# Linear attention and two MLPs on one core: the first attention's steps in one written order, the exponential table fetched at the start

## The chip, the cores and the metric

The kernel runs as one program on one core of a Trainium2 chip. The metric is the device time of one execution in microseconds. Three executions of the kernel before took 1090.41, 1093.3 and 1094.17 us; the median, 1093.3 us, is the time that the change is compared with.

## What is computed

Four batches, 8 heads, 576 positions, head dimension 64, 128 features. Cut to what matters:

```
def phi(x):
    proj = einsum('bhsd,df->bhsf', x, w_phi)
    proj = proj - max(abs(proj), axis=-1, keepdims=True)
    return concatenate([exp(proj), exp(-proj)], axis=-1)
q_p, k_p = phi(q), phi(k)
kv  = einsum('bhsf,bhsd->bhfd', k_p, v)
z   = sum(k_p, axis=2)
num = einsum('bhsf,bhfd->bhsd', q_p, kv)
den = einsum('bhsf,bhf->bhs', q_p, z)[..., None] + 1e-6
x   = (num / den) as (2304, 512)
h   = x @ w_in                      # 512 -> 2048
x   = maximum(0.01 * h, h) @ w_out  # 2048 -> 512
g   = x @ w_gate                    # 512 -> 1536
out = (g * sigmoid(g) * (x @ w_val)) @ w_out2
```

## The kernel before

The work goes batch by batch (b = 0 to 3). A batch's attention gives `x` of 512 rows and 576 columns, held as a rounded part `xh` and a rest `xl`; both MLPs then run on these columns as a list of units, each a group of matmuls for one block of 128 features. The attention of batch b+1 is spread between the units of batch b. Only the attention of batch 0 has nothing beside it but the first conversions of weights: it is the opening, and the change is about it alone.

A head pair j (four of them) is two heads side by side. In the opening the keys of a pair are handled as three groups of key tiles (two, two and one tile of 128 positions), twelve groups p = 0 to 11 in all. For each, TensorE projects the keys (`first_k`, L431), VectorE takes the largest absolute value (L441) and subtracts it (L442, recorded at the helper `sub`, L60), ScalarE makes both exponentials (L446, L447), and TensorE multiplies them with the values and ones (`k_back`, L225) into one bank that sums a pair. ScalarE copies that bank out (`k_z`, `kvh`).

The queries of a pair are handled in two halves t of 288 columns, eight groups g = 2j + t. For each, TensorE projects both heads (`q_p`, L339) and VectorE takes the largest absolute value within blocks, transposed (L344). Then the maximum is turned by TensorE (`q_m_t`, L356), reduced, split in two parts and spread over the rows by VectorE (L361 to L369), subtracted by a matmul into the projection's bank (`q_exp`, L379), and ScalarE makes both exponentials (L381, L382). `q_num` multiplies with `kvh` on TensorE (L399) and copies the denominators on ScalarE (L402). `q_fin` transposes them, takes the reciprocal, transposes back, multiplies (VectorE, L407 to L417), casts to `xh` on ScalarE (L69) and subtracts for `xl` on VectorE (L60).

The order of these steps is made in two stages. `first_steps` gives each piece a time on a scale of its own and emits the pieces in that order; then the scheduler, which works with estimated times, orders the instructions of each engine once more. Only those that carry the token "opening" keep the order in which they were emitted: the exponentials, the copies and casts by `cp`, the denominators, and one step of each weight's conversion (L570), all on ScalarE. TensorE and VectorE follow the scheduler.

A weight arrives as 64-bit numbers and is converted by two steps on ScalarE and three on VectorE (three and two for the second MLP): an absolute value with a scale (L570), a conversion of the low half (L572), shift, merge and add on VectorE (L580, L581, L586), then a rounded part by ScalarE (L596) and the rest by VectorE (L60). Raw weights and the first MLP's converted weights share five buffers named `wi`. Four weights, those of the first four units, are converted in the opening (`split_first`). After it `split_next` converts about two a unit.

The loads of keys, queries and constants go through SP's queue, w_phi and the values of the first two head pairs through ScalarE's. Each loading engine issues in order. Names in the views: `raw` and `pk` are keys and queries, `xh` and `xl` at first also values, `wo` the key features, `mk` their maxima, `pm` and `pa` banks of PSUM, `acc` the maxima spread over rows, `dn` the denominators, `es` a tile for constants and later for results of units. The matmuls of units have line 660.

Of the kernel before, what the change touches and what calls it, by code (L numbers as in the profile page):

```python
# [17 lines left out]
P = 128  # L18
# [21 lines left out]


@with_exitstack
def linear_attention_two_mlps(ctx: ExitStack, tc, qT, kT, vt, w_phi, w1, w2, wg, wv, w3, cst, out):
# [15 lines left out]
    def sub(o, a, b):  # L59
        dve.tensor_tensor(out=o, in0=a, in1=b, op=ALU.subtract)  # L60
# [3 lines left out]
    def in_opening(i):  # L64
        if opening[0]:
            tc.stamp_issue_order_token(i.ins, "opening")

    def cp(o, a):
        in_opening(act.activation(o, a, AF.Copy))  # L69
# [22 lines left out]
    def query_constants():  # L92
        s = signs.pop()
        for t in mm:
            dve.tensor_scalar(out=t, in0=s[:, 0, 0:32], scalar1=0.0, scalar2=None, op0=ALU.mult)
        dve.tensor_scalar(out=ones, in0=s[:, 0], scalar1=0.0, scalar2=1.0, op0=ALU.mult, op1=ALU.add)
        dve.tensor_copy(sel, s)
# [11 lines left out]
    def warm_up():  # L109
        zero = T([P, 2 * F], F32, "es", 5)  # L110
        pool.memset(zero, 0.0)
        ps = bk(0)
        for i in range(5):
            pe.matmul(ps[:, 0 : 2 * F], zero[:, 0:F], zero, start=True, stop=True)
# [15 lines left out]
    def load_k(b, j):  # L130
        raw["k", b, j] = t = T([P, S], F32, *(("pk", 5) if b == 0 and j > 1 else ("raw", 2)))
        if b or j:
            nc.sync.dma_start(out=t, in_=kT[b, j])
        else:
            nc.scalar.dma_start(out=wbd.rearrange("p h f -> p (h f)"), in_=w_phi)
            for c in (slice(0, 256), slice(256, S)):
                nc.sync.dma_start(out=t[:, c], in_=kT[b, j][:, c])
        if whole(b):
            for s in range(0, NST, 2):
# [4 lines left out]
                q = nc.scalar if b == 0 and j < 2 else nc.sync  # L144
                q.dma_start(out=t[:, :, :, 0, :], in_=vt[b, j, :, s : s + n])
# [19 lines left out]
    def v_split(b, j):  # L165
# [4 lines left out]
        for st in (slice(0, 2), slice(2, NST)):  # L170
            i = act.activation(t[:, st, :, 0, :], v[:, st], AF.Copy)
            tc.stamp_issue_order_token(i.ins, "opening")
            sub(t[:, st, :, 1, :], v[:, st], t[:, st, :, 0, :].bitcast(F32))

    def k_front(b, j, s):
# [12 lines left out]
        mk = T([P, 2], F32, "mk", 2)  # L188
# [27 lines left out]
    def k_back(b, j, s):  # L216
# [4 lines left out]
        if whole(b):  # L221
            v = vaug.pop((b, j, s))
            for h in range(2):
                for a in range(2):
                    pe.matmul(  # L225
# [6 lines left out]
                    )  # L232
            return
        v = vhl[b, j][:, s]
        for h in range(2):
            for i, part in enumerate((fh, fl)):
                pe.matmul(  # L237
# [6 lines left out]
                )  # L244
# [85 lines left out]

    def q_p(b, j, t):

        c = slice(HT * t, HT * t + HT)
        m = tops[t][:, 0 : 2 * NB].rearrange("p (h k) -> p h k", h=2)
        for h in range(2):
            bank = pt[b, j, h, t] = bk(b)
            ps = bank[:, 0:HT]
            if b == 0:
                pe.matmul(ps, wbd[:, h], raw["q", b, j][:, c], start=True, stop=True)  # L339
            else:  # L340
                a = qs[b, j][h][:, c]
                pe.matmul(ps, wst_h, a, start=True, stop=False)
                pe.matmul(ps, wst_l, a, start=False, stop=True)
            dve.tensor_reduce(  # L344
                out=m[:, h],
                in_=ps.rearrange("p (k i) -> p k i", i=32),
                axis=AX.X,
                op=ALU.max,
                apply_absolute_value=True,
                apply_transpose=True,  # L350
            )

    def q_m_t(b, j, t):

        turned = pt[b, j, 1, t][:, HT : HT + P]
        pe.matmul(  # L356
            turned, tops[t], ident, is_transpose=True, start=False, stop=True, skip_group_check=True
        )
        turned = turned[0 : 2 * NB]
        top = T([2 * NB, 32], F32, "top", 2)  # L360
        dve.tensor_reduce(out=top, in_=turned.rearrange("r (g i) -> r i g", g=4), axis=AX.X, op=ALU.max)  # L361
        x = mm[t]
        hi = x[0 : 2 * NB]
        dve.tensor_copy(hi, top)
        sub(x[32 : 32 + 2 * NB], top, hi.bitcast(F32))
        if t == 0:
            mrow[b, j] = T([P, 2 * NB, 32], F32R, *(("mrow", 1) if b else ("acc", 4)))
        r = mrow[b, j][:, NB * t : NB * t + NB]
        dve.tensor_tensor(  # L369
            out=r,  # L370
            in0=x.bitcast(F32).rearrange("p (o i) -> p o i", o=1).to_broadcast([P, NB, 32]),
            in1=mask.rearrange("p (k o) -> p k o", o=1).to_broadcast([P, NB, 32]),
            op=ALU.mult,
        )

    def q_exp(b, j, h, t):
        ps = pt.pop((b, j, h, t))[:, 0:HT]
        r = mrow[b, j][:, NB * t : NB * t + NB].rearrange("p k i -> p (k i)")
        pe.matmul(ps, sel[:, h], r, start=False, stop=True, skip_group_check=True)  # L379
        f = T([P, 2, HT], F32, "ff" if b else ("ff", "fh", "fl")[(2 * t + h + j) % 3], 3)  # L380
        in_opening(act.activation(f[:, 0], ps, AF.Exp))  # L381
        in_opening(act.activation(f[:, 1], ps, AF.Exp, scale=-1.0))  # L382
# [8 lines left out]
    def q_num(b, j, h, t):  # L391
# [6 lines left out]
        for i, (w, x) in enumerate(ops):  # L398
            pe.matmul(ps, w, x, start=(i == 0), stop=(i == len(ops) - 1))  # L399
        if h == 0:  # L400
            dn[b, j, t] = T([P, HT], F32, "dn", 2)
        in_opening(act.activation(dn[b, j, t][D * h : D * h + D], ps[D:P], AF.Copy, bias=1e-6))  # L402

    def q_fin(b, j, t):
        d = dn.pop((b, j, t))
        t1 = T([P, HT // 32, 32], F32, "t1", 1)
        dve.transpose(out=t1.rearrange("p a b -> p (a b)"), in_=d)  # L407
        rc = T([P, HT // 32, 1], F32, "rc", 1)
        dve.reciprocal(out=rc, in_=t1[:, :, 0:1])
        rb = T([P, HT // 32, 32], F32, "rb", 1)  # L410
        dve.transpose(out=rb, in_=rc.to_broadcast([P, HT // 32, 32]))
        rb = rb.rearrange("p a b -> p (a b)")
        x = T([P, HT], F32, "xf", 1)
        for h in range(2):
            o = slice(D * h, D * h + D)
            ps = qn.pop((b, j, h, t))
            dve.tensor_tensor(out=x[o], in0=ps[0:D, 0:HT], in1=rb[o], op=ALU.mult)  # L417
# [4 lines left out]
        cp(xh[b, j][:, c], x)  # L422
        sub(xl[b, j][:, c], x, xh[b, j][:, c].bitcast(F32))
# [3 lines left out]
    def first_k(j, s, n):  # L427
        ps = bk(0)
        for i in range(n):
            o = slice(OFF[s + i], OFF[s + i] + P)  # L430
            pe.matmul(  # L431
                ps[:, 2 * F * i : 2 * F * i + 2 * F],
                raw["k", 0, j][:, o],
                wbd.rearrange("p h f -> p (h f)"),
                start=(i == 0),
                stop=(i == n - 1),
                skip_group_check=True,
            )
        pv = ps[:, 0 : 2 * F * n].rearrange("p (r f) -> p r f", f=F)
        mk = T([P, 2 * n], F32, "mk", 2)  # L440
        dve.tensor_reduce(out=mk, in_=pv, axis=AX.X, op=ALU.max, apply_absolute_value=True)  # L441
        f = T([P, n, 2, 2, F], F32, "wo", 5)  # L442
        d = f.rearrange("p n h a f -> p (n h) a f")
        m = mk.rearrange("p (r o) -> p r o", o=1).to_broadcast([P, 2 * n, F])
        sub(d[:, :, 1], pv, m)
        in_opening(act.activation(d[:, :, 0], d[:, :, 1], AF.Exp))  # L446
        in_opening(act.activation(d[:, :, 1], d[:, :, 1], AF.Exp, scale=-1.0))  # L447
        for i in range(n):
            ff[0, j, s + i] = f[:, i]

    def first_back(j, s, n):
        for i in range(n):
            k_back(0, j, s + i)
        if s + n == NST:
            k_z(0, j)

    def first_steps():

        events = []

        def at(time, fn, *args):
            events.append((time, len(events), lambda: fn(*args)))

        for i, (j, s, n) in enumerate(pairs):
            at(i, first_k, j, s, n)
            at(i + 1.4, first_back, j, s, n)
        for g in range(2 * NP):
            j, t = divmod(g, 2)
            base = 2 + 1.3 * g
            last = max(base + 2.05, 3 * j + 3.5 + 0.4 * t)  # L470
            at(base + 0.1, q_p, 0, j, t)
            at(base + 0.7, q_m_t, 0, j, t)
            for h in range(2):
                at(base + 1.25 + 0.1 * h, q_exp, 0, j, h, t)
                at(last + 0.2 * h, q_num, 0, j, h, t)
            at(last + 0.25, q_fin, 0, j, t)
        steps = [[] for _ in range(int(max(e[0] for e in events)) + 1)]
        for time, _, fn in sorted(events, key=lambda e: e[:2]):
            steps[int(time)].append(fn)
        return steps  # L480
# [80 lines left out]
    def w_to_f32(key):  # L561


# [6 lines left out]
        i = act.activation(t, high.bitcast(F32), AF.Abs, scale=REBIAS)  # L570
        tc.stamp_issue_order_token(i.ins, "opening")
        act.activation(low, low.bitcast(U32), AF.Copy, scale=2.0**-29)  # L572
        if key[0] in "gv3":

            act.activation(high, high.bitcast(F32), AF.Prelu, scale=2.0**-20, alpha=2.0**100)
            dve.scalar_tensor_tensor(
                out=ti, in0=ti, scalar=3, in1=high, op0=ALU.logical_shift_left, op1=ALU.bitwise_or
            )
# [626 lines left out]
```

## Time and profile before

| what | value |
|---|---|
| median of three executions | 1093.3 us |
| the profiled execution | 1097.21 us |
| its span, first to last instruction | 1095.3 us |
| mean granted TensorE clock (1.00 is full) | 0.983 |
| TensorE busy | 1059.4 us, 97% |
| VectorE busy | 798.1 us, 73% |
| ScalarE busy | 650.7 us, 59% |

The views are these. The page gives busy time by engine and by group of instructions. The windows give each engine's busy time in a stretch, with the number of instructions (x), and the granted clock. The waits say who stood idle for whom: total, number of times, longest. The timeline lists instructions by start and duration; a bracket gives the idle time before one and what ended it. PE is TensorE, DVE VectorE, ACT ScalarE, POOL GpSimd; ACTq and SPq are the queues that issue transfers. A matmul leaves two records in most of these views, so a count of records is twice a count of matmuls where the operands are of full fp32.

### The profile page before, as it was taken

The numbers are of one execution on the slowest core, as the hardware profiler recorded it, in microseconds if no ns is written. First come the engines' busy times: TensorE is split into PE (matmuls) and PEld (weight loads), VectorE is DVE, ScalarE is ACT, GpSimd is POOL, SyncE is SP. The second block draws the span as 40 slices with busy tenths as digits, with TensorE's granted clock in tenths as the row PEclk, the third lists the DMA queues.
The fourth block names the chain that finished last, engine by engine and source line by source line (L and its number), as shares of the span: only waits on it lengthen the run. The fifth ranks groups of instructions, "written<-read, shape, count | busy, mean of one in ns | idle before, by whom it ended". The sixth has DMA issues, their size and how long they took to land.

```text
span 1095.3 us, 20408 instructions
## 1 busy us (share of the span) xinstructions
PE 1059.4 (97%) x7642; PEld 1031.3 (94%) x7642; DVE 798.1 (73%) x1730; ACT 650.7 (59%) x1443; POOL 21.8 (2%) x57
## 2 busy tenths in 40 slices
PE   8779899999999999999999999999999999999998
PEld 7658899998989999999999999999999999999998
DVE  4665888999888988868776865858878742368473
ACT  4436988789896788846553366755444234336441
POOL 1000010000000000000000000000000000000000
PEclk9889899999999999999999999999999999999999
DMA  8102887656775697776463375536968757657542
GB/s 246 36 22 76 327 291 239 213 197 233 231 247 165 238 354 291 279 294 224 155 232 127 134 280 211 193 119 253 322 242 311 281 171 277 239 173 265 197 148 89
DMA packets 101492, 236.19 MB, mean 216 GB/s; under 512 B 19857, under 2 KB 35985, under 8 KB 101393
## 3 DMA queue, kind: packets, MB, share of 16 engines
q1 hardware_dynamic: 94560, 219.41, 57.4%
q0 software_dynamic: 4032, 14.68, 3.6%
q8 instruction: 61, 1.00, 0.4%
q10 hardware_dynamic: 2800, 0.79, 0.3%
q14 instruction: 39, 0.31, 0.1%
HBM read 169.30 MB, written 65.54 MB: 214 GB/s over the span
## 4 chain that ended last, share of the span: by engine, by line
PE 80%; DMA 6%; DVE 4%; ACT 2%; issue 1%; SPq 0%; DVEq 0%; ACTq 0%
PE pm L660 56%; PE pa L786 8%; PE pm L786 4%; PE pa L399 3%; PE pa L184 2%; PE pa L237 2%; PE pa L225 1%; DMA wi<-in_w_dram 1%; DMA wi<-in_wg_dram 1%; DMA wo<-parts 1%; DMA wi<-parts 1%; DMA wr<-kept 1%; DMA sums<-wr 1%; DMA vhl<-parts 1%; PE pa L379 0%
## 5 line engine op out<-in xcount | busy, mean ns | idle before, releaser
L660 PE MATMUL pm<-xh,wi 128*128 128x288 f32 x1664 | 353.7, 299 | 3.3 <-DVE wi L60 1.1
L660 PE MATMUL pm<-gp,wo 128*128 128x288 f32 x2256 | 340.5, 298 | 0.9 <-ACT gp L69 0.4
L660 PEld LDWEIGHTS pm<-gp,wo 128*128 128x128 f32 x2256 | 313.8, 189 | 3.3 <-ACT gp L69 1.4
L660 PEld LDWEIGHTS pm<-xh,wi 128*128 128x128 f32 x1664 | 273.0, 189 | 6.7 <-DVE wi L60 1.9
L660 PE MATMUL pm<-xl,wi 128*128 128x288 f32 x832 | 247.1, 298 | 0.0
L660 PEld LDWEIGHTS pm<-xl,wi 128*128 128x128 f32 x832 | 157.4, 189 | 0.4
L727 DVE TENSOR_TENSOR acc<-pm,acc 128x288 f32<-128x288 f32 x160 | 69.9, 451 | 48.0 <-PE pm L660 47.2
L60 DVE TENSOR_TENSOR gp<-es,gp 128x576 fp32r<-128x576 f32 x94 | 70.5, 750 | 25.9 <-ACT gp L69 25.2
L69 ACT ACTIVATE gp<-es 128x576 fp32r<-128x576 f32 x94 | 64.7, 690 | 28.4 <-DVE es L708 23.2
L60 DVE TENSOR_TENSOR wi<-wr,wi 128x512 fp32r<-128x512 f32 x96 | 65.1, 683 | 14.1 <-ACT wi L596 13.4
L596 ACT ACTIVATE wi<-wr 128x512 fp32r<-128x512 f32 x96 | 60.2, 638 | 21.0 <-DVE wr L60 5.3
L786 PE MATMUL pm<-xh,wi 128*128 128x288 f32 x272 | 62.6, 296 | 1.8 <-ACT xg L69 0.8
L60 DVE TENSOR_TENSOR fl<-ff,fh 128x512 fp32r<-128x512 f32 (+1 forms) x72 | 51.1, 712 | 10.2 <-ACT fh L69 9.8
L572 ACT ACTIVATE wi<-wi 128x512 int32<-128x512 uint32 x68 | 46.4, 685 | 17.7 <-DMA wi<-in_wg_dram 9.4
L570 ACT ACTIVATE wr<-wi 128x512 f32<-128x512 f32 x68 | 46.4, 683 | 15.6 <-DMA wi<-in_w_dram 5.8
L586 DVE TENSOR_TENSOR wr<-wr,wi 128x512 uint16<-128x512 uint16 x68 | 51.4, 755 | 1.2
L786 PEld LDWEIGHTS pm<-xh,wi 128*128 128x128 f32 x272 | 46.4, 188 | 2.9 <-DVE mk L189 1.1
L402 ACT ACTIVATE dn<-pa 64x288 f32<-64x288 f32 x64 | 26.0, 406 | 38.7 <-PE pa L399 37.8
L69 ACT ACTIVATE fh<-ff 128x512 fp32r<-128x512 f32 (+1 forms) x72 | 47.4, 664 | 0.9
L688 ACT ACTIVATE es<-pm 128x288 f32<-128x288 f32 x72 | 29.7, 421 | 24.4 <-PE pm L786 16.5
L69 ACT ACTIVATE acc<-pm 128x288 f32<-128x288 f32 x64 | 26.2, 417 | 26.5 <-PE pm L660 26.5
L708 DVE SCALAR_TENSOR_TENSOR es<-pm,es 128x288 f32<-128x288 f32 x72 | 31.9, 447 | 12.8 <-PE pm L660 12.3
(212 smaller groups left out, 2087.0 us busy)
## 6 DMA issues: line engine op xcount, KB each, us to landing
wo<-parts SPq DMA_DIRECT2D x77, 512.0 KB, 6.2
wi<-parts SPq DMA_DIRECT2D x68, 512.0 KB, 5.5
parts<-wi SPq DMA_DIRECT2D x56, 512.0 KB, 4.4
wi<-in_w_dram SPq DMA_DIRECT2D x44, 512.0 KB, 5.3
wr<-kept SPq DMA_DIRECT2D x64, 256.0 KB, 4.2
parts<-wo POOLq DMA_DIRECT2D x28, 512.0 KB, 5.7
kept<-wr SPq DMA_DIRECT2D x40, 256.0 KB, 4.5
wi<-in_wg_dram SPq DMA_DIRECT2D x12, 512.0 KB, 4.6
```

Source lines behind the costliest of these rows:

```text
L60: dve.tensor_tensor(out=o, in0=a, in1=b, op=ALU.subtract)
L69: in_opening(act.activation(o, a, AF.Copy))
L399: pe.matmul(ps, w, x, start=(i == 0), stop=(i == len(ops) - 1))
L570: i = act.activation(t, high.bitcast(F32), AF.Abs, scale=REBIAS)
L572: act.activation(low, low.bitcast(U32), AF.Copy, scale=2.0**-29)
L586: dve.tensor_tensor(out=t16, in0=t16, in1=e16, op=ALU.add)
L596: i = act.activation(t[:, 0], r, AF.Copy)
L660: m = pe.matmul(ps, w, x[:, c], start=(i == 0), stop=(i == n - 1))
L688: act.activation(o, i, AF.Prelu, alpha=0.01)
L708: dve.scalar_tensor_tensor(out=g[:, c], in0=ps, scalar=0.5, in1=g[:, c], op0=ALU.mult, op1=ALU.mult)
L727: dve.tensor_tensor(out=acc[o][:, t], in0=ps, in1=acc[o][:, t], op=ALU.add)
L786: m = pe.matmul(ps, a, b, start=start and n == 0, stop=stop and n == 5, skip_group_check=True)
```

## The change

The opening gets a written order: a string of 305 step names, and a dictionary that gives each name its code. Every instruction of a step on TensorE, VectorE and ScalarE is stamped with the token "opening" (`keep`), so that the scheduler may not exchange two of them on one engine. The old functions are cut into single steps for it. In the names, a K step belongs to a key group: KP projects, KR takes the largest, KS subtracts, KE and KF are the two exponentials, KB the product, KZ the copy of a pair's bank. A Q step belongs to a query group and, with a second digit, to a head: QP projects, QR takes the largest, QT turns, QA reduces, QB and QC split, QD spreads, QS subtracts, QE and QF are the exponentials, QN the product, DN the denominators. FT, FR, FB and FX are the transposes, the reciprocal and the multiplication, XH and XL the cast and the rest. C0 makes the constants; CA to CH are the steps of one of the first four weights.

Besides: the exponential is called once on a tile of zeros ahead of all else, so that its table is fetched there; three of the six value loads of ScalarE's queue go through SP's; `mk` has four buffers in place of two; in the main loop too the first two steps of a weight's conversion on ScalarE (all three for the second MLP) are stamped, where only the first was.

```
+OPENING = """
+KP0 KP1 KR0 KS0 KP2 KR1 QP00 KE0 KS1 QP01 KF0 KR2 QP10 KE1 KS2 QR01 KB0 KF1 QR00 KE2 C0 KF2
+KP3 KB1 KR3 KS3 KE3 KP4 KF3 QT0 KB2 KR4 QA0 QB0 KB3 KS4 KZ0 QC0 QR10 KE4 QD0 KF4 KP6 CA0
...
+FT6 XH5 FR6 FB6 QN70 DN71 XL5 FX6 DN70 XH6 FT7 XL6 FR7 FB7 FX7 XH7 XL7
+"""
...
     def sub(o, a, b):
-        dve.tensor_tensor(out=o, in0=a, in1=b, op=ALU.subtract)
+        keep(dve.tensor_tensor(out=o, in0=a, in1=b, op=ALU.subtract))
...
-    def in_opening(i):
+    def keep(i):
         if opening[0]:
             tc.stamp_issue_order_token(i.ins, "opening")
 
+    def after_opening(i):
+        tc.stamp_issue_order_token(i.ins, "opening")
...
-                q = nc.scalar if b == 0 and j < 2 else nc.sync
-                q.dma_start(out=t[:, :, :, 0, :], in_=vt[b, j, :, s : s + n])
+                q = act if b == 0 and j == 0 else nc.sync
+                i = q.dma_start(out=t[:, :, :, 0, :], in_=vt[b, j, :, s : s + n])
+                if q is act:
+                    keep(i)
...
-        i = act.activation(t, high.bitcast(F32), AF.Abs, scale=REBIAS)
-        tc.stamp_issue_order_token(i.ins, "opening")
-        act.activation(low, low.bitcast(U32), AF.Copy, scale=2.0**-29)
+        after_opening(act.activation(t, high.bitcast(F32), AF.Abs, scale=REBIAS))
+        yield
+        after_opening(act.activation(low, low.bitcast(U32), AF.Copy, scale=2.0**-29))
+        yield
...
-    warm_up()
+    zero = warm_up()
     load_k(0, 0)
+    keep(act.activation(zero[:, 0:2], zero[:, 0:2], AF.Exp))
...
-    steps = first_steps()
-
-    for i, todo in enumerate(steps):
-        for fn in todo:
-            fn()
-        if i == 1:
-            query_constants()
-        if i == 4:
+    ops = opening_ops()
+    for name in OPENING.split():
+        ops.pop(name)()
+        if name == "KP2":
             load_q(0, 3)
             ahead(loaded, w_load, 4)
-        if i in (4, 6, 8, 10):
-            split_first()
-        if i == 11:
-            split_constants()
+        if name == "QP71":
             load_k(1, 0)
+    conv[0] = done[0] = 4
+    split_constants()
     opening[0] = False
```

Three places of the resulting order. First ScalarE's start, where the table is loaded. Before:

```order
L145 DMA xl_107<-in_vt_dram 128x4x64
L145 DMA xh_110<-in_vt_dram 128x4x64
L145 DMA xl_113<-in_vt_dram 128x2x64
L446 ACT_TABLE_LOAD
L446 ACTIVATE wo_147<-wo_147 128x4x128
L447 ACTIVATE wo_147<-wo_147 128x4x128
```

Now:

```order
L167 DMA xh_97<-in_vt_dram 128x2x64
L1234 ACT_TABLE_LOAD
L1234 ACTIVATE es_79<-es_79 128x2
L541 ACTIVATE wo_151<-wo_151 128x4x128
L544 ACTIVATE wo_151<-wo_151 128x4x128
```

The table load stands behind three value loads where it stood behind six, and ahead of a call on a tile of its own (`es_79`, the zeros of the warm-up) where it stood ahead of the first key exponential.

Second, VectorE's start: maxima and subtractions of the first key groups, and the constants (L95 to L97, now L116 to L118). Before:

```order
L441 TENSOR_REDUCE mk_145<-pm_142 128x4
L95 TENSOR_SCALAR mm_77<-es_102 128x32
L95 TENSOR_SCALAR mm_78<-es_102 128x32
L60 TENSOR_TENSOR wo_147<-pm_142,mk_145 128x4x128
L96 TENSOR_SCALAR ones<-es_102 128x128
L441 TENSOR_REDUCE mk_154<-pm_151 128x4
L97 CAST sel<-es_102 128x256
```

Now:

```order
L532 TENSOR_REDUCE mk_149<-pm_143 128x4
L78 TENSOR_TENSOR wo_151<-pm_143,mk_149 128x4x128
L532 TENSOR_REDUCE mk_165<-pm_146 128x4
L78 TENSOR_TENSOR wo_170<-pm_146,mk_165 128x4x128
L532 TENSOR_REDUCE mk_175<-pm_153 128x2
L78 TENSOR_TENSOR wo_180<-pm_153,mk_175 128x2x128
L370 TENSOR_REDUCE cst_sb<-pm_172 128x9
L370 TENSOR_REDUCE cst_sb<-pm_167 128x9
L116 TENSOR_SCALAR mm_77<-es_103 128x32
```

Each subtraction follows its maximum, and the constants come behind the first three key groups and the first query maxima.

Third, VectorE at the second query group's maximum (`top`, QA1 to QD1), where the cast of the projection's constants (`wbd_h`, from a second load `es_740`) has its place now:

```order
L394 TENSOR_REDUCE top_303<-pm_277 18x32
L397 CAST mm_78<-top_303 18x32
L78 TENSOR_TENSOR mm_78<-top_303,mm_78 18x32
L123 CAST wbd_h<-es_740 128x256
L406 TENSOR_TENSOR acc_246<-mm_78,cst_sb 128x288
L698 TENSOR_SCALAR wr_290<-wr_290 128x512
```

This cast is not stamped; the scheduler has put it between the split of the maximum and its spread.

## Rows read from the trace of the kernel before

**Rows 1.** The page: busy us, share of the span, instructions, by engine.
```profile
PE 1059.4 (97%) x7642; PEld 1031.3 (94%) x7642; DVE 798.1 (73%) x1730; ACT 650.7 (59%) x1443; POOL 21.8 (2%) x57
```

**Rows 2.** Windows: length, busy PE, PEld, DVE, ACT, POOL; clock, DMA share, GB/s.
```profile
0.00:8.50 8.50, 6.47 (x22) 5.12 (x22) 0.90 (x4) 0.94 (x1) 3.09 (x17) 1.00 0.86 226
8.50:20.00 11.50, 10.21 (x56) 8.82 (x57) 7.02 (x20) 6.05 (x14) 0.32 (x1) 0.85 1.11 346
20.00:85.00 65.00, 50.19 (x232) 39.59 (x231) 43.41 (x109) 30.75 (x70) 1.14 (x4) 0.84 0.13 41
85.00:101.00 16.00, 15.10 (x85) 13.69 (x85) 7.29 (x20) 8.42 (x26) 0.00 (x0) 0.89 0.16 50
...
118.00:200.00 82.00, 81.93 (x600) 81.02 (x601) 71.17 (x138) 71.98 (x170) 7.27 (x15) 0.97 0.77 269
```

**Rows 3.** Waits, 0 to 118 us: us in total, times, longest.
```profile
DVE mk L441 <- PE pm L431: 16.4, 6, 5.8
ACT xh L69 <- DVE xf L417: 16.1, 7, 3.3
DVE t L407 <- ACT dn L402: 14.6, 5, 6.9
```

**Rows 4.** Timeline, 100 to 121 us: start, duration, engine, line, operation.
```profile
101.14 0.51 ACT L69 ACTIVATE xh<-xf 128x288 fp32r<-128x288 f32 x1
...
104.46 0.33 SPq L556 DMA_DIRECT2D wi<-in_w_dram  x1
...
105.64 1.36 SPq L556 DMA_DIRECT2D wi<-in_w_dram  x3
...
112.66 0.67 ACT L570 ACTIVATE wr<-wi 128x512 f32<-128x512 f32 x1 [0.51 <-DMA wi<-in_w_dram]
...
117.38 0.63 ACT L596 ACTIVATE wi<-wr 128x512 fp32r<-128x512 f32 x1
...
118.07 0.61 PE L660 MATMUL pm<-xh,wi 128*128 128x288 f32 x1 [0.70 <-ACT wi L596]
```

**Rows 5.** Timeline, the first 12 us.
```profile
1.10 3.83 PE L114 MATMUL pm<-es 128*128 128x256 f32 x10 [1.10 <-POOL es L111]
...
5.83 0.69 DVE L441 TENSOR_REDUCE mk<-pm 128x4 f32<-128x512 f32 x1 [5.83 <-PE pm L431]
...
7.45 0.39 SPq L145 DMA_DIRECT2D xh<-in_vt_dram  x1
7.56 1.28 ACT L446 ACT_TABLE_LOAD   x1 [7.56 <-DMA xl<-in_vt_dram]
...
8.29 0.27 DVE L95 TENSOR_SCALAR mm<-es 128x32 fp32r<-128x32 f32 x2 [1.77 <-DMA es<-in_cst_dram]
8.47 0.68 DVE L60 TENSOR_TENSOR wo<-pm,mk 128x512 f32<-128x512 f32 x1
...
9.19 0.63 ACT L446 ACTIVATE wo<-wo 128x512 f32<-128x512 f32 x1 [0.34 <-DVE wo L60]
```

**Rows 6.** Windows of ten microseconds each.
```profile
30.00:40.00 10.00, 6.11 (x27) 4.62 (x26) 8.18 (x21) 5.38 (x13) 0.31 (x1) 0.91 0.23 70
60.00:70.00 10.00, 6.77 (x17) 4.06 (x18) 6.43 (x15) 4.84 (x11) 0.00 (x0) 0.60 0.07 26
110.00:120.00 10.00, 7.17 (x42) 6.37 (x41) 9.07 (x20) 9.49 (x25) 0.62 (x2) 0.83 0.99 361
```

**Rows 7.** The chain that ended last, in order of time: start, us, what.
```profile
128.96 0.89 PE pa L225 x8
```

**Rows 8.** DMA, 0 to 40 us: busy tenths by microsecond; issues, KB, us to landing.
```profile
DMA  0289999999999999999999300000007206005000
...
wi<-in_w_dram SPq DMA_DIRECT2D x4, 512.0 KB, 6.1
```

**Rows 9.** Timeline of TensorE, 58.5 to 66 us.
```profile
60.70 0.54 PE L379 MATMUL pm<-acc,sel 128*128 128x288 f32 x2 [2.41 <-DVE acc L369]
```

**Rows 10.** The page, costliest groups: count, busy us, mean ns, idle before.
```profile
L572 ACT ACTIVATE wi<-wi 128x512 int32<-128x512 uint32 x68 | 46.4, 685 | 17.7 <-DMA wi<-in_wg_dram 9.4
```

More of the change, by code (lines that the diff above doesn't have):

```diff
@@ L329, in q_split, with top_of, q_p_h @@
         sub(s1[0:D], r[D:P], s1[D:P].bitcast(F32))
+    def top_of(t, h):
+        m = tops[t][:, 0 : 2 * NB].rearrange("p (h k) -> p h k", h=2)
+        return m[:, h]
+    def q_p_h(b, j, h, t):
+        c = slice(HT * t, HT * t + HT)
+        bank = pt[b, j, h, t] = bk(b)
+        ps = bank[:, 0:HT]
+        if b == 0:
+            keep(pe.matmul(ps, wbd[:, h], raw["q", b, j][:, c], start=True, stop=True))
+        else:
+            a = qs[b, j][h][:, c]
+            keep(pe.matmul(ps, wst_h, a, start=True, stop=False))
+            keep(pe.matmul(ps, wst_l, a, start=False, stop=True))
@@ L331, in q_p, with q_top @@
+    def q_top(b, j, h, t):
+        keep(dve.tensor_reduce(
+            out=top_of(t, h),
+            in_=pt[b, j, h, t][:, 0:HT].rearrange("p (k i) -> p k i", i=32),
+            axis=AX.X,
+            op=ALU.max,
+            apply_absolute_value=True,
+            apply_transpose=True,
+        ))
     def q_p(b, j, t):
-        c = slice(HT * t, HT * t + HT)
-        m = tops[t][:, 0 : 2 * NB].rearrange("p (h k) -> p h k", h=2)
         for h in range(2):
[L336 to L366, printed above, removed]
+            q_p_h(b, j, h, t)
@@ L451, in first_back, with q_xl @@
[L451 to L466, printed above, removed]
+        cp(xh[b, j][:, c], xfs[b, j, t])
+    def q_xl(b, j, t):
+        c = slice(HT * t, HT * t + HT)
+        sub(xl[b, j][:, c], xfs.pop((b, j, t)), xh[b, j][:, c].bitcast(F32))
@@ L478, in first_steps @@
-        for time, _, fn in sorted(events, key=lambda e: e[:2]):
-            steps[int(time)].append(fn)
-        return steps
+                for name, fn in (
+                    ("QP", q_p_h),
+                    ("QR", q_top),
+                    ("QS", q_shift),
+                    ("QE", q_pos),
+                    ("QF", q_neg),
+                    ("QN", q_prod),
+                    ("DN", q_den),
+                ):
+                    ops[f"{name}{g}{h}"] = later(fn, 0, j, h, t)
@@ new lines, in opening_ops @@
+            for name, fn in (
+                ("QT", q_turn),
+                ("QA", q_max),
+                ("QB", q_hi),
+                ("QC", q_lo),
+                ("QD", q_row),
+                ("FT", q_t1),
+                ("FR", q_rc),
+                ("FB", q_rb),
+                ("FX", q_x),
+                ("XH", q_xh),
+                ("XL", q_xl),
+            ):
+                ops[f"{name}{g}"] = later(fn, 0, j, t)
+        ops["C0"] = query_constants
+        for c in range(4):
+            turns = conversion(order[c])
+            for name in ("CA", "CB", "CD", "CE", "CF", "CG", "CH"):
+                ops[f"{name}{c}"] = later(next, turns, None)
@@ L482, in q_steps @@
+        return ops
     def q_steps(b):
@@ L561, in w_to_f32, with to_f32 @@
     def w_to_f32(key):
+        for _ in to_f32(key):
+            pass
+    def to_f32(key):
         if key not in w64:
@@ L596, in to_wtile, with conversion @@
         i = act.activation(t[:, 0], r, AF.Copy)
-        tc.stamp_issue_order_token(i.ins, "weights")
+        if not opening[0]:
+            tc.stamp_issue_order_token(i.ins, "weights")
+        sub(t[:, 1], r, t[:, 0].bitcast(F32))
+    def conversion(key):
+        yield from to_f32(key)
+        yield
+        r = wf.pop(key)
+        t = parts_tile(key)
+        cp(t[:, 0], r)
+        yield
         sub(t[:, 1], r, t[:, 0].bitcast(F32))
```

226 lines of the change are left out of this document (147 added, 79 removed).

## The prediction

> **What bounds the kernel now.** I read the page's shares first [rows 1]: TensorE is busy 97% of the 1095.3 us span, no other engine above 73%. A change that only reorders work can gain where TensorE waits, or runs at a low clock, and nowhere else. So next the busy time by stretch [rows 2]. From 118 us on TensorE has 81.93 of 82 us, and the later stretches are alike (slices of 9 in the page). Before it stands the first attention, and there nothing is full: from 20 to 85 us VectorE is busy 43.41 of 65 us (67%), TensorE 50.19 at a granted clock of 0.84, ScalarE 30.75. Third, the waits up to 118 us [rows 3]: VectorE for TensorE's projections (16.4 us) and for ScalarE's copy of the denominators (14.6), ScalarE for VectorE's result (16.1). They wait for one another in turn: the stretch is bound by hand-offs, not by an engine. Last, its end in order of time [rows 4]: the last cast of the attention's result on ScalarE starts at 101.14, and until the units run without a pause there is a chain behind it. The fifth weight of layer 1 is loaded at 104.46, three more at 105.64; ScalarE waits for those until 112.66, and the fifth weight's cast stands behind them in its order, at 117.38; TensorE starts the fifth unit at 118.07. That is 16.9 us after the cast.
>
> **The change, part by part.**
> *The work itself* stays: the same matmuls, reductions, exponentials, weight conversions. What moves is when the last cast (the step XH7) starts, so that is the term to size.
>
> VectorE's work: 0.90 + 7.02 + 43.41 + 7.29 = 58.6 us are busy up to 101 us [rows 2], the first reduction starting at 5.83 [rows 5]. About 0.9 us of it (low half of the projection's constants, `wbd_l`, `wst_l`) goes behind the attention, so I take 58. TensorE's work: 6.47 + 10.21 x 0.85 + 50.19 x 0.84 + 15.10 x 0.89 = 70.8 us at full clock, of which 3.8 are the warm-up [rows 5] and some 8 the units begun early, so about 59. Neither can end the attention before some 65 to 70 us; with two engines nearly equal, how tightly the sequence interleaves them decides.
>
> Filled to f, VectorE reaches XH7 at 5.83 + 58/f. The ends: f = 0.67, what it has from 20 to 85 us, gives 92.4 us; f = 0.91, its best ten microseconds near here (110 to 120: 9.07) [rows 6], gives 69.6 us. I take 0.82, the best ten microseconds inside the attention itself (30 to 40: 8.18) [rows 6], because the tail of the sequence, like its head, still consists of dependent steps: 58/0.82 = 70.7, XH7 at 76.5 us, **24.6 us earlier**.
>
> *What follows XH7.* The chain of 16.9 us starts from this cast: the conversion of the first layer-2 weight comes after it on ScalarE in both orders, the fifth weight's load waits for that conversion's buffer, and the cast of the fifth weight keeps its place behind three conversions. So it moves along whole. TensorE fills less of it: by the order it has done 7 key projections and 20 key products of the second attention at the fifth unit, where it had done 8 and 24 by the order before. A matmul leaves two records; eight records of a key product take 0.89 us [rows 7], 0.11 each, and one of a projection has twice the columns, about 0.22. So 8 x 0.11 + 2 x 0.22 = 1.3 us are still to do. **Minus 1.3.** Behind that TensorE is full, so the shift reaches the end: 24.6 - 1.3 = 23.3 us.
>
> *The table.* The load takes 1.28 us, at 7.56, since ScalarE's six DMA issues before it wait for their queue; the first exponential starts at 9.19 [rows 5]. What held it was VectorE: the subtraction started at 8.47, behind two small steps that waited for the constants until 8.29. Now the subtraction follows its reduction directly (5.83 + 0.69 + 0.68 = 7.2), and the table, behind the warm-up's last read of the same tile (1.10 + 3.83 = 4.93), is there at 6.21. Alone the fetch is worth nothing, and without it the earlier subtraction would wait 1.6 us. The two together are 1.9 us, a part of the 24.6 and not added to it. The Trainium skill, "ScalarE: Activation LUTs", section "What ACT_TABLE_LOAD costs", puts a drain of about 1.38 us behind the 1.28 us load. By it the first exponential could not have started before 10.2 us; the row says 9.19, so the measurement decides against it. With the drain the new first exponential would start at 7.6, 0.4 us late, and the sum would be 22.9.
>
> *Loads.* Three value loads (the second head pair's) leave ScalarE's queue for SP's, at about 0.4 us an issue (0.39 at 7.45 [rows 5]), and everything behind them on SP is issued some 1.2 us later: the query and key loads, four weights, the projection's second copy. Two steps in the sequence now stand where they could be met: ScalarE's first weight conversion (CA0) ahead of the first query exponentials, and VectorE's cast of `wbd` between QC1 and QD1. The weights took 6.1 us to land at the median, and the DMA engines are nine tenths busy up to 22 us and idle from 23 [rows 8], so everything had landed by then. With 1.2 us on top it is there by 24.2. At f = 0.82 VectorE reaches its cast with some 13 us of work done, at 5.83 + 13/0.82 = 21.7. So from 0 to 2.5 us of wait, with QD1 and the next query products behind it; I take 0, since the products before it keep TensorE fed, and keep 2.5 for the range.
>
> *Buffers and later order.* `mk` with four buffers instead of two takes away a wait on VectorE only: nothing. In the main loop the first two conversion steps of a weight on ScalarE must now keep the sequence (rival D).
>
> The profiled execution took 1097.2 us (span 1095.3 and 1.9 around it), 0.4% above the median of 1093.3. The shift is the same against either: 1097.2 becomes 1073.9, and the median 1093.3 - 23.3 = **1070.0 us**.
>
> **The rivals.**
> *A, the forecast.* Bounds from f = 0.91 (101.14 - 69.6 - 1.3 = 30.2 us, 1063.1) to about f = 0.75 (5.83 + 77.3 = 83.1; 16.7 us, 1076.6).
>
> *B, the hand-offs stay.* The written order ties three engines step by step, so one late step holds the other two, TensorE idles in short pieces and its clock falls. For it: the granted clock is 0.60 from 60 to 70 us [rows 6], and TensorE had waited 2.41 us for VectorE when its next query product started at 60.70 [rows 9], and 59 us of its work at 0.84 are 70 us, as long as the whole attention should take. Against it: the sequence puts other pairs' key products (16 records, twice 0.89 us [rows 7]) between a query product and what it waits for. Price: f = 0.67 as now, XH7 at 92.4, 8.7 - 1.3 = 7.4 us: 1085.9. The Trainium skill, "TensorE: Matmul & The Clock Gate", section "Loop structure matters more than you think", speaks for this rival: waits between bursts of matmuls put the clock back to 1.2 GHz, the lower of its levels.
>
> *C, given back at the fifth unit.* SP issues in order. If the loads for the fifth unit still came at 105 us, because buffer loads of the second attention stand ahead of them in SP's order, TensorE would only wait longer for 118 us: no change, 1093. Against it: those buffers are freed by key and query projections (KP11, QP71) that lie well before the end of the attention.
>
> *D, slower.* The conversion's second step (L572, 68 of them at 685 ns [rows 10]) could so far run whenever ScalarE was free, and some ran ahead of the first step; now all keep the sequence. If each of the 64 outside the attention makes its weight 0.685 us later and TensorE waits for it, that costs 43.8 us: 1093.3 - 23.3 + 43.8 = 1113.8. It ends on the slow side once more than 34 of them (23.3/0.685) reach TensorE. For it: ScalarE is busy 71.98 of 82 us from 118 to 200. Against it: TensorE has 81.93 of the same 82, so the weights are there in time with something to spare.
>
> **How the numbers follow.** A 0.70, B 0.18, C 0.06, D 0.06. Differences within 0.3% (3.3 us) are about what a measurement of this kernel can't tell from none. A and B are faster: 0.88; C the same: 0.06; D slower: 0.06. The range takes A's low bound (1063, one less for a part of the chain that may shrink) and reaches to where most of B begins, with the 2.5 us of a late load: 1062 to 1084.
>
> **What would show it.** Right: the last cast of the attention's result starts at 70 to 83 us; VectorE above 75% busy from 20 us to there; the first exponential near 7.3; the fifth unit some 16 us after the last cast; TensorE full from there. B: a clock below 0.9 through the attention and VectorE at two thirds. C: three weight loads still near 105. D: idle time of TensorE before layer-1 units from 120 to 300 us, put down to ScalarE's casts. I am wrong in the main term if the last cast starts after 84 us, and wrong in the reasoning if it starts in time and the end does not move by as much.

## The result and the profile after

The changed kernel takes 1065.35 us (median of 4 executions, 1062.66 to 1067.45) beside 1092.11 us for the kernel before on the same chip (1090.41 to 1094.17): ratio 0.9753, 95% interval 0.9722 to 0.9783. The forecast was 1070.0 us, within 1062 to 1084. The profiled execution took 1064.56 us, its span 1062.7.

The page's shares, to be held against [rows 1]:

```profile
PE 1040.7 (98%) x7642; PEld 1019.6 (96%) x7642; DVE 796.4 (75%) x1730; ACT 649.0 (61%) x1444; POOL 21.4 (2%) x57
```

VectorE and ScalarE have the work they had. TensorE has the same 7642 records, but 1040.7 us of work in place of 1059.4: 18.7 us less, and 22.0 us of idle time in place of 35.9. Windows cut at the start of the fifth unit show where (length, busy PE, PEld, DVE, ACT, POOL; clock, DMA share, GB/s). Before:

```profile
0.00:118.07 118.07, 96.21 (x490) 80.46 (x491) 71.48 (x178) 60.82 (x145) 6.03 (x26) 0.88 0.37 115
118.07:1095.30 977.23, 963.22 (x7152) 950.82 (x7152) 726.65 (x1553) 589.87 (x1299) 15.78 (x31) 1.00 0.65 228
```

After:

```profile
0.00:89.36 89.36, 81.36 (x481) 69.68 (x481) 69.94 (x178) 59.46 (x142) 6.04 (x26) 1.00 0.48 148
89.36:1062.70 973.34, 959.34 (x7162) 949.89 (x7162) 726.43 (x1553) 589.56 (x1303) 15.40 (x31) 1.00 0.65 229
```

The stretch up to the fifth unit is 28.7 us shorter: 14.9 us are TensorE's busy time and 13.9 us its idle time (21.9 to 8.0). Nine records fewer lie ahead of the unit (481 for 490), about 1.3 us by [rows 7]; the other 13.6 us are the same work at a mean granted clock of 1.00 in place of 0.88. One group of matmuls with the same count and shape shows it (groups of TensorE in the two stretches: count, busy us, mean ns of one, idle before), first before, then after:

```profile
L399 PE MATMUL pa<-ff,kvh 128*128 128x288 f32 x24 | 8.8, 500 | 0.0
```

```profile
L459 PE MATMUL pa<-ff,kvh 128*128 128x288 f32 x24 | 6.8, 406 | 0.0
```

The rest of the program differs by 3.9 us; the profiled execution of before lies 5.1 us above its median, so little of that need be the change.

The windows inside the opening, after (beside [rows 2, 6]):

```profile
8.50:20.00 11.50, 10.90 (x80) 10.01 (x80) 7.57 (x20) 7.08 (x13) 0.00 (x0) 1.00 1.10 348
20.00:30.00 10.00, 9.13 (x56) 7.61 (x54) 7.31 (x21) 9.37 (x22) 0.32 (x1) 1.00 0.32 107
30.00:40.00 10.00, 7.69 (x46) 6.33 (x46) 9.57 (x26) 4.34 (x11) 0.31 (x1) 1.00 0.06 15
40.00:50.00 10.00, 9.38 (x54) 7.70 (x53) 9.85 (x21) 8.45 (x20) 0.52 (x2) 1.00 0.55 178
...
60.00:70.00 10.00, 9.71 (x55) 8.20 (x54) 7.79 (x21) 5.66 (x15) 0.00 (x0) 1.00 0.11 31
...
80.00:90.00 10.00, 8.42 (x63) 7.75 (x62) 9.50 (x22) 10.00 (x27) 0.83 (x3) 1.00 1.03 357
```

From 8.5 to 30 us TensorE (and at last ScalarE) is nearly full and VectorE waits; from 30 to 50 us VectorE is full and TensorE has gaps, the larger up to 40; from 60 to 80 TensorE is the fuller again; from 80 us ScalarE is full. The waits up to 118 us (us in total, times, longest) stood at 16.4, 16.1 and 14.6 us in [rows 3]:

```profile
DVE mk L532 <- PE pm L518: 10.7, 4, 6.9
ACT xh L90 <- DVE xf L492: 4.5, 3, 2.7
DVE t L476 <- ACT dn L465: 3.6, 3, 1.6
```

The first contains the 6.9 us before the first reduction. Last, the timeline at the start and at the end of the opening (start, duration, engine, line, operation), beside [rows 4, 5]:

```profile
5.82 1.28 ACT L1234 ACT_TABLE_LOAD   x1 [5.82 <-PE pm L135]
7.12 0.20 ACT L1234 ACTIVATE es<-es 128x2 f32<-128x2 f32 x1
8.37 0.63 ACT L541 ACTIVATE wo<-wo 128x512 f32<-128x512 f32 x1 [1.05 <-DVE wo L78]
...
73.59 0.45 ACT L90 ACTIVATE xh<-xf 128x288 fp32r<-128x288 f32 x1
...
77.19 1.77 SPq L671 DMA_DIRECT2D wi<-in_w_dram  x4
...
88.56 0.74 ACT L716 ACTIVATE wi<-wr 128x512 fp32r<-128x512 f32 x1
...
89.36 0.40 PE L790 MATMUL pm<-xh,wi 128*128 128x288 f32 x1 [1.14 <-ACT wi L716]
```

The last cast (XH7) starts at 73.59 us, 27.55 earlier than before; loads, conversion and fifth unit follow it at 3.6, 15.0 and 15.8 us.

### The profile page after: what moved, and what is told of

It reads as the page before. It is cut to its first block, busy times and chain, and to the rows that moved or that the text cites. A ratio compares the mean times of both kernels' runs of the same rounds, so it can differ in the third digit from the quotient of the medians.

```text
span 1062.7 us, 20417 instructions
## 1 busy us (share of the span) xinstructions
PE 1040.7 (98%) x7642; PEld 1019.6 (96%) x7642; DVE 796.4 (75%) x1730; ACT 649.0 (61%) x1444; POOL 21.4 (2%) x57
## 4 chain that ended last, share of the span: by engine, by line
PE 78%; DVE 8%; ACT 7%; DMA 5%; issue 1%; SPq 0%; POOL 0%; ACTq 0%; DVEq 0%; POOLq 0%
PE pm L790 53%; PE pa L916 9%; PE pm L916 5%; PE pa L459 3%; PE pa L260 2%; PE pa L207 2%; PE pa L248 2%; DMA wr<-kept 2%; ACT wr L687 1%; DMA wi<-in_w_dram 1%; ACT wi L689 1%; DMA wi<-parts 1%; DMA wi<-in_wv_dram 1%; DMA wi<-in_wg_dram 1%; DVE wr L706 1%
## 5 line engine op out<-in xcount | busy, mean ns | idle before, releaser
L706 DVE TENSOR_TENSOR wr<-wr,wi 128x512 uint16<-128x512 uint16 x68 | 51.1, 754 | 0.9
L90 ACT ACTIVATE acc<-pm 128x288 f32<-128x288 f32 x64 | 27.3, 448 | 25.0 <-PE pm L790 24.6
```

The costliest lines, as they stand in the source:

```text
L90: keep(act.activation(o, a, AF.Copy))
L706: keep(dve.tensor_tensor(out=t16, in0=t16, in1=e16, op=ALU.add))
```

## The experiments

All ratios are against the kernel before on the same chip. Two things change in the opening: which sequence is written, and that three engines keep it where only ScalarE did. E1, E2 and E5 separate them.

**E1: the new sequence, held on ScalarE alone.**

```
 def keep(i):
-    if opening[0]:
+    if opening[0] and i.ins.engine == mybir.EngineType.Activation:
```

> Same written sequence, but only ScalarE's instructions keep it; TensorE and VectorE are ordered by the scheduler again, as in the kernel before. Theory H (the hold on all three engines is what counts): the scheduler's estimates exchange steps of TensorE and VectorE against ScalarE's fixed order, the hand-offs come back, VectorE falls to about 70% from 20 us on, the last cast of the attention's result starts at 85 to 100 us in place of 73.6, and the time is 1077 to 1092 us. Theory S (the sequence is what counts, and any order made from it is good): last cast by 78 us, time within 4 us of 1065. I expect H, nearer its low end: about 1080.

Measured: 1073.65 us, ratio 0.9822 (0.9802 to 0.9842); last cast at 82.66. Between the theories: nearly three quarters of the gain are there without the hold. One place where the rest is lost (timeline of E1, 26 to 40 us, and the window from 30 to 40):

```profile
28.57 0.67 DVE L700 SCALAR_TENSOR_TENSOR wr<-wi,wr 128x512 int32<-128x512 int32 x1
...
30.35 0.70 DVE L706 TENSOR_TENSOR wr<-wr,wi 128x512 uint16<-128x512 uint16 x1
...
31.33 0.66 DVE L78 TENSOR_TENSOR wo<-pm,mk 128x512 f32<-128x512 f32 x1
...
32.13 0.72 PE L363 MATMUL pm<-pk,wbd 128*128 128x288 f32 x2 [3.64 <-DVE wo L78]
...
36.51 1.17 PE L459 MATMUL pa<-ff,kvh 128*128 128x288 f32 x2
...
30.00:40.00 10.00, 6.66 (x15) 4.31 (x16) 7.00 (x19) 3.16 (x8) 0.00 (x0) 0.67 0.16 61
```

The scheduler put steps of weight conversions (L700, L706) and constants ahead of a key subtraction; TensorE waited 3.64 us for the bank that it frees, and then ran a half query product in 1.17 us that takes 0.65 elsewhere: the granted clock was 0.67 from 30 to 40 us. E1 lets go of TensorE and VectorE together; which of the two holds matters wasn't tried.

**E2: the old sequence, held on all three engines.**

```
-KP0 KP1 KR0 KS0 KP2 KR1 QP00 KE0 KS1 ...
+KP0 KR0 KS0 KE0 KF0 KP1 KR1 KS1 KE1 KF1 KB0 C0 KP2 ...
```

> The order in which the kernel before emitted its pieces, written as the sequence and held on all three engines; all else is as in the changed kernel. Theory S (the particular interleaving counts): steps of one group stand behind one another, so a held order makes the engines wait for each other at every step; VectorE at 67% or less, last cast at 95 us or later, time 1088 to 1105 us. Theory H (it is the hold): last cast below 82 us, time below 1074. I expect S, about 1095.

Measured: 1103.81 us, ratio 1.0101 (1.0083 to 1.0120), last cast at 115.57. Holding an order is no gain by itself: on the old sequence it costs 1% where on the new one it brings 0.7%. In the old sequence the steps of one group stand behind one another, so an engine that keeps it waits at the hand-offs; TensorE's longest three waits are 7.06, 6.95 and 5.59 us (shown under E6).

**E5: the old sequence, held on ScalarE alone (the two edits above together).**

> The changed kernel with the old sequence, held on ScalarE alone: order and hold of the kernel before, with the early table, the moved value loads, four mk buffers and the stamped conversion steps left in. If these small parts are worth nothing, as I priced them, the time is that of the kernel before, 1094 within 4 us, and the last cast of the attention stands near 101 us. If they carry a part of the gain, it is below 1088; if they cost something, above 1098. I expect 1094.

Measured: 1093.12 us, ratio 0.9995 (0.9976 to 1.0014), last cast at 104.16. So all other parts of the change together (early table, moved loads, `mk`, stamped conversions) make no difference that can be measured on the old sequence; the gain is the new sequence and its hold. On the new sequence E3, E4 and E9 take back one part each; `mk` with two buffers wasn't run there.

**E3: without the early exponential.**

```
-    keep(act.activation(zero[:, 0:2], zero[:, 0:2], AF.Exp))
```

> Without the early call of the exponential; the table is loaded ahead of the first key exponential again. In the changed kernel the first key exponential starts at 8.37 us and waits for VectorE's subtraction, and ScalarE's queue has only three value loads ahead of the table. Theory Q (a load of the table waits for nothing but the instructions ahead of it): it starts by about 6.5 us, is there by 7.8, and nothing changes: 1065 within 1 us. Theory T (the fetch was worth its length): the first exponential starts 1.3 us later or more and the end moves by as much, 1066 to 1067. I expect Q.

Measured: 1065.84 us, ratio 0.9747 (0.9723 to 0.9770), as with it. ScalarE's timeline of E3:

```profile
2.22 0.53 ACTq L167 DMA_DIRECT2D xh<-in_vt_dram  x1
2.78 1.28 ACT L541 ACT_TABLE_LOAD   x1 [2.78 <-issue]
8.73 0.63 ACT L541 ACTIVATE wo<-wo 128x512 f32<-128x512 f32 x1 [4.67 <-DVE wo L78]
```

Theory Q, and more: the load waits here for the issues ahead of it and for nothing else. Without the early call it starts at 2.78; with it, at 5.82, behind the warm-up that reads the same tile. What had held the table until 7.56 in the kernel before [rows 5] were the three value loads that the change moved away: the last of them was issued there from 7.16 to 7.54.

**E4: those three value loads back on ScalarE's queue**, behind the early call.

```
-    q = act if b == 0 and j == 0 else nc.sync
+    q = act if b == 0 and j < 2 else nc.sync
```

> The values of the second head pair go through ScalarE's queue again (three issues of about 0.4 us behind the early exponential at 7.1 us, so until about 8.3), SP's queue is three issues shorter. If the queue of the loads counted: the first key exponential waits for the issues instead of VectorE and starts at 8.4 to 8.7, and the time rises by up to 0.5 us; on the other side the weights and the projection's constants land up to 1.2 us earlier, which gains nothing as long as no step waits for them. I expect no difference: 1065 within 1 us.

Measured: 1063.44 us, ratio 0.9731 (0.9710 to 0.9751). No difference: the first exponential starts at 8.61 and waits for VectorE. E3 and E4 show that either part can be taken back while the other stands; both taken back with the new sequence wasn't tried.

**E9: the conversions' later steps without token behind the opening** (rival D).

```
-    after_opening(act.activation(low, low.bitcast(U32), AF.Copy, scale=2.0**-29))
+    keep(act.activation(low, low.bitcast(U32), AF.Copy, scale=2.0**-29))
```

(and the same for the third step).

> The changed kernel, but behind the opening the second step of a weight's conversion on ScalarE (and the third for the second MLP) carries no token, as before the change. By rival D these kept steps would cost 0.685 us each wherever TensorE waits for them: then the time falls, by up to a few us. By my forecast they are hidden under TensorE: 1065 within 1.5 us.

Measured: ratio 0.9751 (0.9720 to 0.9782), that of the changed kernel (0.9753); the medians, 1068.02 and 1065.35, were measured beside different executions of the kernel before. Rival D costs nothing that the interval, some 7 us wide, can show.

**E7 and E8: which engine sets the opening now?** E7 takes the maximum of six key groups twice (the first two lines), E8 projects their keys twice (the others).

```
+    if p in (3, 4, 6, 7, 9, 10):
+        ops[f"KR{p}"] = later(twice, largest, p, n)
...
-    for i in range(n):
+    for i in (0, 1, 0, 1) if p in (3, 4, 6, 7, 9, 10) else range(n):
```

> The changed kernel with the maximum taken twice for six of the key groups (3, 4, 6, 7, 9, 10): 6 x 0.69 = 4.1 us more for VectorE between 13 and 65 us, no other work. If VectorE still sets when the first attention ends, the last cast starts 3 to 4 us later (76.5 to 77.7) and the time rises by as much, to 1068.5 to 1069.5; if TensorE sets it, by under 1.5 us. I expect about 3.

> The changed kernel with the key projection done twice for the same six key groups: 6 x 0.87 = 5.2 us more for TensorE (two matmuls of 256 columns, 0.87 us from the start of one projection to what follows it), VectorE's work unchanged. TensorE has some 5 us of gaps from 8.5 to 73.6 us and is full behind. If VectorE sets the end of the attention, half of the added work or more falls into the gaps: the time rises by 0 to 2.6 us. If TensorE sets it: 4 to 5.2 us, to 1069.5 to 1070.5. I expect about 4, because from 8.5 to 27 us TensorE has no gap and VectorE waits for it.

Measured: E7 1068.28 us, ratio 0.9766 (0.9732 to 0.9801); E8 1065.74, ratio 0.9755 (0.9716 to 0.9793). The last casts, first of E7, then of E8:

```profile
76.58 0.45 ACT L90 ACTIVATE xh<-xf 128x288 fp32r<-128x288 f32 x1
```

```profile
76.45 0.45 ACT L90 ACTIVATE xh<-xf 128x288 fp32r<-128x288 f32 x1
```

VectorE's added 4.1 us move the last cast by 3.0, TensorE's added 5.2 us by 2.9. Other runs with this sequence (E3, E4, E9) have it at 73.38 to 73.95, so both shifts are clear, but 2.9 and 3.0 aren't to be told apart. Neither engine binds alone: 0.73 and 0.55 of an added microsecond arrive at the end of the opening. E7's median lies 2.9 us above the changed kernel's, E8's 0.4; the intervals are 7 to 8 us wide and decide neither, so my expectation for E8's total isn't confirmed.

**E6 and E10: what the clock costs.** In E2 three waits are followed by matmuls at half clock. The timeline of TensorE in E2 has two of them here (the third, at 95.95, is like the first), and the window behind the first wait has a granted clock of 0.50:

```profile
52.89 1.30 PE L362 MATMUL pm<-pk,wbd 128*128 128x288 f32 x2 [7.06 <-DVE wo L77]
53.98 3.62 PE L247 MATMUL pa<-xh,wo 128*128 128x128 f32 x16
...
72.95 2.29 PE L458 MATMUL pa<-fl,kvh 128*128 128x288 f32 x4 [5.59 <-ACT kvh L89]
...
52.89:57.60 4.71, 4.71 (x19) 4.42 (x20) 0.72 (x2) 2.46 (x6) 0.00 (x0) 0.50 0.00 0
```

E6 put idle work into these waits, in the spare columns of a bank in use.

```
+    for i in range(24):
+        keep(pe.matmul(bank()[:, HT : HT + P], wbd[:, 0], wbd[:, 0],
+                       start=False, stop=True, skip_group_check=True))
```

> The old sequence held on all three engines (1103.8 us), with 24 matmuls of 128 columns, whose result nobody reads, put on TensorE ahead of each of the three instructions for which it waited longest (7.06 us at 52.9, 5.59 at 72.95, 6.95 at 95.95). They take some 5.3 us each at full clock (0.22 us apiece, by the key products), so they lie in the waits. Theory C (a wait costs a second time, since TensorE goes on at half clock after it): the matmuls after the waits, now 1.30, 3.62, 2.29, 2.12 us and so on where others of their kind take 0.65, 1.95, 1.13, run at full clock, and the time falls by 5 to 9 us, to 1095 to 1099. Theory W (the waits alone cost, what runs after them is hidden): 1104 within 2 us, or more by as much as the added matmuls stick out of the waits. I expect C, about 1097.

Measured: 1116.42 us, ratio 1.0199 (1.0166 to 1.0232). A miss, and the timeline says why:

```profile
54.40 8.29 PE L592 MATMUL pm<-wbd 128*128 128x128 f32 x48 [6.83 <-DVE cst_sb L369]
```

Two of the three added groups waited for VectorE's maximum of their own bank and stood behind the wait instead of in it. This one began at half clock and took 8.29 us for what takes 5.52 (the other 7.11; granted clock 0.65 from 54.4 to 62.5 us). E10 gives them a bank of their own:

```
+    spare = bk()
+    for i in range(24):
+        keep(pe.matmul(spare[:, 0:P], wbd[:, 0], wbd[:, 0], start=True, stop=True))
```

> The old sequence held on all three engines (1103.8 us), with 24 matmuls that nobody reads ahead of each of TensorE's three longest waits (QP41, QN40, QP71), now into a bank of their own, so that they wait for no other engine (in the first try two of the three groups stood behind VectorE's maximum of their bank, at half clock, and lengthened the path). Theory C (a wait costs a second time through the clock): what follows the three waits runs at full clock (0.65 in place of 1.30 for the query projections, 1.95 for 3.62 for the key products, 1.13 for 2.29 for the query products), 8 to 9 us less TensorE time on the path, and the time falls to 1095 to 1099. Theory W (only the waits count): 1104 within 2 us. I expect C.

Measured: 1100.34 us, ratio 1.0055 (1.0034 to 1.0076), beside 1.0101 (1.0083 to 1.0120) for E2; last cast at 106.20 in place of 115.57. Timeline of TensorE in E10:

```profile
45.54 5.52 PE L593 MATMUL pa<-wbd 128*128 128x128 f32 x48
52.80 0.72 PE L362 MATMUL pm<-pk,wbd 128*128 128x288 f32 x2 [1.74 <-DVE wo L77]
53.36 1.95 PE L247 MATMUL pa<-xh,wo 128*128 128x128 f32 x16
...
70.30 1.24 PE L458 MATMUL pa<-fl,kvh 128*128 128x288 f32 x4 [0.23 <-ACT kvh L89]
```

72 matmuls whose result nobody reads, 16.6 us of work, make the opening 9.4 us shorter: 0.72, 1.95 and 1.24 us where E2 has 1.30, 3.62 and 2.29, and a granted clock of 1.00 up to 118 us. Theory C holds for the opening. Its total was a near miss, 1100.34 for 1095 to 1099: of the 9.4 us, 3.5 show in the median (about 5 by the ratios), so a part is given back behind the opening, in a place that I didn't isolate. In the profiled executions the part behind the last cast takes 990.8 us in E10 and 986.4 in E2.

**E11 and E12: other sequences.** The rows of the changed kernel show that TensorE is full while VectorE waits (8.5 to 30 us) and has gaps afterwards. Two sequences of the same 305 steps move key projections ahead of key products (KP3 and KP4 ahead of KB0 in E11, say).

```
-KP0 KP1 KR0 KS0 KP2 KR1 QP00 KE0 KS1 QP01 KF0 KR2 QP10 KE1 KS2 QR01 KB0 ...
+KP0 KP1 KR0 KP2 KS0 QP00 KR2 KS2 KR1 KP3 KR3 KS1 KE0 KP4 KR4 KF0 KB0 ...
```

> Another sequence of the same 305 steps, nothing else changed. It was looked for with the durations of the rows of the changed kernel: each step put as early as its inputs, its buffer and the step before it on its engine allow. So reckoned the changed kernel's sequence has its last cast at 68.9 us (the trace: 73.6, with units' matmuls in between) and TensorE 5.8 us of gaps; this one 63.7 and 0.5, mainly since key projections stand before key products of earlier groups, which fill TensorE's gaps from 28 to 37 us instead. If the gaps of the opening are what is left to gain, the last cast starts at 68 to 70 and the time is 1059 to 1062. If what follows (ScalarE full from 80 to 100 us up to the fifth unit's weight) takes it back, the last cast moves and the time stays at 1063 to 1066. I expect 1061.

> A second sequence found in the same way from another start (reckoned last cast 63.9, gaps of TensorE 0.8 us). If the reckoning from the rows holds, it does as well as the other within 1 us; if what a sequence is worth hangs on things the reckoning leaves out (landing of loads, the scheduler's units in between), the two differ by more.

Measured: 1058.96 us, ratio 0.9663 (0.9634 to 0.9692), and 1059.39 us, ratio 0.9667 (0.9639 to 0.9696): both some 6 us below the changed kernel by the medians, 9 to 10 by the ratios, and the fastest here; the intervals don't touch its own. Last casts at 67.64 and 68.64. Windows of E11:

```profile
8.50:20.00 11.50, 11.44 (x73) 9.99 (x72) 10.93 (x28) 8.01 (x17) 0.32 (x1) 1.00 1.10 349
...
30.00:40.00 10.00, 9.84 (x56) 8.03 (x55) 9.87 (x25) 8.45 (x20) 0.32 (x1) 1.00 0.13 39
...
0.00:83.46 83.46, 79.60 (x480) 69.20 (x480) 68.52 (x178) 58.47 (x142) 6.06 (x26) 1.00 0.51 160
83.46:1057.20 973.74, 960.04 (x7162) 950.14 (x7162) 726.59 (x1553) 589.26 (x1303) 15.43 (x31) 1.00 0.66 229
```

VectorE does 10.93 us of work by 20 us where it did 7.57, TensorE's gap from 30 to 40 us is closed, and the fifth unit starts 5.9 us earlier. Up to it TensorE now idles 3.9 us, so what a sequence can still take from its waits is less than that.

## Why the prediction was right, and where it wasn't

*When the last cast starts.* Forecast 76.5, measured 73.59; VectorE's row for the stretch from its first reduction to the last cast:

```profile
6.92:73.59 66.67, 61.35 (x363) 51.52 (x362) 56.19 (x144) 42.60 (x99) 1.46 (x5) 1.00 0.39 118
```

56.2 us of work where I took 58, f = 0.84 where I took 0.82, and a start 1.1 us later. The term came out at 27.55 in place of 24.6 us: the mechanism was right, its size 3 us too small.

That f came so near is in part luck. I took it from the best ten microseconds of the old order and didn't work it out from the new sequence, and f is a matter of the sequence. With the same hold, the same row of E2 gives 60.34/108.24 = 0.56 and that of E11 54.70/61.26 = 0.89:

```profile
7.33:115.57 108.24, 74.36 (x378) 62.05 (x377) 60.34 (x146) 44.97 (x106) 1.46 (x5) 0.86 0.23 72
```

```profile
6.38:67.64 61.26, 60.09 (x363) 51.40 (x362) 54.70 (x144) 41.84 (x100) 1.46 (x5) 1.00 0.43 131
```

TensorE, with the units' matmuls in between, is fuller than the engine that I sized by: 61.35 of 66.67 us in the changed kernel, 60.09 of 61.26 in E11.

*What the term is made of* I saw only half. I counted the gain as VectorE filled better and treated the clock as a rival's affair. Of the 28.7 us up to the fifth unit 13.6 are TensorE's clock. The two aren't separate causes: a wait costs its own length and then slows what follows, as E10 shows, where useless matmuls fill the waits and what follows them runs at full clock. The Trainium skill, "TensorE: Matmul & The Clock Gate", section "Loop structure matters more than you think", says that a loop in which matmuls stand behind long waits (its example is a DMA's) leaves them at the lower clock. E2 and E10 agree, with 3.62 and 1.95 us for the same 16 records.

*The chain behind it* was to move whole, 16.9 us; it is 15.8 (89.36 - 73.59) and ends on the fifth weight's cast as before, 1.1 us better than forecast. The 1.3 us for work of the second attention that isn't done yet fits: its key products and projections have 40 and 14 records ahead of the unit where they had 48 and 16, ten fewer as forecast. The count of all records falls by nine because one more of the units' stands there.

*The table.* This step failed. That "without it the earlier subtraction would wait 1.6 us" was wrong: without the early call the load starts at 2.78 (E3), long before the exponential behind that subtraction needs it. That the first exponential started at 8.37 and not at the expected 7.3 has another reason: the first reduction started at 6.92 in place of 5.83, and the exponential follows it by 1.45 us, about as reckoned. I had taken the 7.56 us of [rows 5] as it stood and hadn't asked what remains of it once half of the issues ahead of it are gone. The price of the error was small because VectorE, not the table, releases that exponential. The drain that the Trainium skill ("ScalarE: Activation LUTs", section "What ACT_TABLE_LOAD costs") gives as about 1.38 us isn't in the changed kernel's trace either: the load ends at 7.10, the next instruction starts at 7.12. The section has it for every switch to a different set of functions; each of these programs loads a table only once, so no run here shows such a switch.

*Loads, `mk`, later order.* Nothing expected, nothing found (E4, E9, and for `mk` E5, on the old sequence alone); VectorE's cast of `wbd_h` starts at 24.36 without a wait.

*The rivals.* B would have left the clock low: it is 1.00 all through the opening. C would have left the loads near 105: they start at 77.19. D is E9. E2 shows that a slower outcome of the same technique was close by, by the mechanism of B in part: held, the old sequence leaves TensorE idle for 35.0 us up to the last cast, where without the hold it was 21.7 (E5), and the time is 1% longer; the granted clock up to 118 us is 0.87 in both.

*Sum.* With the measured shift of the fifth unit, 28.7 - 1.3 = 27.4 us, the forecast's own working gives 1093.3 - 27.4 = 1065.9; measured 1065.35. The shift reached the end. Of the 4.7 us between forecast and median 4.1 are the sizing of f (with the work of 58 us, 3.0) and of the chain (1.1); the rest is within the spread of the executions.

## What to carry to other kernels

Where several engines hand work to each other and none is full, look at the granted clock of TensorE beside its idle time: here nearly half of what was gained ahead of the fifth unit (13.6 of 28.7 us) lay in the clock of the matmuls behind the waits. A fixed order is worth what the sequence is worth: hold it only once independent work stands between each step and what it waits for, and look for such work where one engine is full while the next stretch has gaps. Before fetching something early, ask what holds it now; it may already be on its way out.

## What the runs showed of the hardware

Three groups of 24 useless matmuls (16.6 us) shortened a stretch by 9.4 us, since the matmuls behind the waits ran at full clock and not at half, the 16 records behind the first in 1.95 us in place of 3.62 (E10 and E2). In the kernel before the warm-up's ten records took 3.83 us [rows 5], in the changed kernel 4.63, and the first reduction came 1.1 us later for it; the work is the same and the cause stays open. Among the experiments the ten records take 4.18 to 4.64 us, and with the very order of the changed kernel (E4, E9) the first reduction starts at 7.16 and 6.70 and the last cast at 73.84 and 73.38, so that much of an opening's end differs from run to run. The column of the granted clock is 1.00 for these first microseconds in every run and doesn't tell the difference.
